# Two attention blocks and a tangent MLP on one core: x read once and transposed on TensorE, the second softmax centred instead of normalised, and a new list-scheduled order

## Chip, cores and metric

One core of one Trainium2 chip. The metric is the time of one execution on the device, in microseconds (us); lower is better. Engines are named as in the profile: PE is TensorE (PEld its weight loads), ACT is ScalarE, DVE is VectorE, POOL is GpSimd, SP is SyncE, which issues all DMAs here. Its DMA queue is worked off in the order of issue, and an issue that waits holds back those behind it.

## What is computed

```python
B, N, m, C = 4, 12480, 32, 128            # x: (B, N, C), inducing: (m, C)
def mab(q, kv):
    s = (q @ kv.transpose(0, 2, 1)) / np.sqrt(C)
    a = np.exp(s - s.max(-1, keepdims=True))
    a /= a.sum(-1, keepdims=True) + 1e-09
    return a @ kv
h = mab(I, x)                              # 32 rows a batch, each a mean over 12480 tokens
t = mab(x, h)                              # 12480 rows a batch, each a mean over 32 rows of h
u = t @ w_in                               # 128 -> 2048
out = (u - np.tanh(u)) @ w_out             # 2048 -> 128
```

The first attention needs all tokens of a batch before `h` is known; the second reads the same tokens again. The rows of `t` lie close together, so both kernels replace the MLP by its tangent at the mean over `h` and apply it to the 32 rows alone: the output is then the second attention's weights times a 32x128 matrix. On the chip a bound on the error of that tangent is worked out. If it is exceeded, a general loop after the main part runs; with these inputs it isn't entered, before or after.

## The kernel before

Every operation is registered with a planner by `add(engine, cost, function, reads, writes, priority)`; `Plan.order` places them by priority, with the costs and the number of free buffers in `PLACES`, and the engines' instruction streams are written out in that order. Within an engine nothing overtakes.

Tokens are handled in steps of up to 1920 (four quarters of `SEG` = 480), seven per batch, the last of 960. The host gives x twice: `xT`, channels on the partitions, and `xn`/`xl`, tokens on the partitions.

- `first(b)`: per step a load of `xT` (L279) and four score products in four column groups (L263, through `scores`), which DVE copies from PSUM with a running maximum (L290). Then the maximum over the batch goes through PE (L299, L307) into `nb`. Per step again: a load of `xn` (L315), the exponential with its sum on ACT (L322), 32x32 transposes on DVE (L326), and 15 accumulating products with `xn` into one PSUM tile (L333). Sum, reciprocal and two small products give `hT` (L342 to L353).
- `linear(b)`: 16 products with a 128x128 piece of `w_in` as weights and 32 moving columns (L367); mean, tanh, slope on DVE and ACT (L379 to L405); 16 products with `w_out` (L416); a copy, a product that repeats the 32 rows four times (L419), a copy.
- `second(b, s)` with `b_chain`: scores with `hT` (L263), transposes on DVE (L455), maximum (L457), subtraction on POOL (L462), exponential on ACT (L464), sum (L467), reciprocal (L472, L473), product on POOL (L475), transposes back (L478), output products in halves of two into `o` (L496), each half evicted by ACT (L502), and one store per step (L505).
- `bound`: 16 products with the absolute `w_out` (L525) and a chain of small DVE operations with the least of all sums, up to `limit`.
- `weight`: the weights come as 64-bit words and are turned into float32 by two ACT, five DVE and two POOL passes per chunk (L218 to L242).

PSUM holds four `ps_m` tiles of one bank and two `o` tiles of two banks. SBUF holds 11 `xT`, 5 `xn` and 3 `ot` buffers; `ot` also takes the raw weights. A load waits until the last reader of its buffer is done, a `COPY` into `ot` until the store of that buffer has landed.

Of the kernel before, what the change touches and what calls it, by code (L numbers as in the profile page):

```python
# [19 lines left out]
NQ = 4  # L20
SEG = 480
KB = SEG // 32
SG = NQ * SEG
SMALL = 0.0625
SERIES = (1.0 / 3.0, -2.0 / 15.0, 17.0 / 315.0)
ROUND = 2.0 ** -24
SLACK = 1.0e-3
# [3 lines left out]

class Buf:


    def __init__(self, make=None, tag=None):
        self.make, self.tag = make, tag
        self.t = None
        self.writer, self.readers, self.left = None, [], 0  # L40

    def get(self):
        if self.t is None:
            self.t = self.make()
        return self.t


class Op:
    def __init__(self, eng, cost, fn, deps, bufs, pri, lag):
        self.eng, self.cost, self.fn, self.deps, self.bufs, self.pri, self.lag = eng, cost, fn, deps, bufs, pri, lag  # L50
        self.start = self.end = None


class Plan:
# [5 lines left out]
    def add(self, eng, cost, fn, reads=(), writes=(), pri=0.0, lag=0.15):  # L60
# [8 lines left out]
        op = Op(eng, cost, fn, deps, list(dict.fromkeys([*reads, *writes])), pri, lag)  # L69
# [9 lines left out]
    def order(self):  # L79
        free = dict(self.places)  # L80
        held = set()
        waiting = {}
        users = {}
# [5 lines left out]
        ready = {}  # L89
        events = []  # L90
        count = itertools.count()
        busy = {}

        def release(op, t):
            ready.setdefault(op.eng, []).append((op.pri, op.n, op))
            ready[op.eng].sort(key=lambda x: x[:2])

        for op in self.ops:
            if not op.deps:
                release(op, 0.0)  # L100
        t, done = 0.0, 0
        while done < len(self.ops):
            for eng, queue in ready.items():
                if busy.get(eng, -1.0) > t:
                    continue
                for k, (_, _, op) in enumerate(queue):
                    need = {}
                    for x in op.bufs:
                        if x.tag and x not in held:
                            need[x.tag] = need.get(x.tag, 0) + 1  # L110
                    if any(free[tag] < c for tag, c in need.items()):
                        continue
                    for x in op.bufs:
                        if x.tag and x not in held:
                            held.add(x)
                            free[x.tag] -= 1
                    queue.pop(k)
                    op.start, busy[eng] = t, t + op.cost
                    op.end = t + op.cost + op.lag
                    heapq.heappush(events, (t + op.cost, next(count), None))  # L120
                    heapq.heappush(events, (op.end, next(count), op))
                    break
            assert events, "no operation can start"
# [553 lines left out]
```

## Time and profile before

| | us |
|---|---|
| median of three runs | 269.49 |
| lowest and highest | 267.08, 271.31 |
| span of the profiled execution, first to last instruction | 267.4 |
| busy: PE, DVE, ACT, POOL | 201.6, 171.4, 97.8, 76.9 |
| first eviction of an output begins | 84.24 |

The device time of the profiled execution is not listed apart from its span; the median is 2.1 us above the span. Busy time counts an instruction from its start to its modelled end, so a PE that is busy is not PE at its best: its instructions take about twice as long when the granted clock is the lower one. The profile reports the granted clock per stretch as a share of full speed (0.50 is 1.2 GHz, 1.00 is 2.4 GHz); in the first 40 us it reads 1.00, while the score products there take as long as they do later at 0.50. An fp32 product appears as two MATMUL instructions, a transpose as one.

### The profile page before, as it was taken

What the parts mean: (1) busy time and instruction counts of PE and PEld (TensorE: products, weight loads), DVE (VectorE), ACT (ScalarE), POOL (GpSimd) and SP (SyncE); (2) the same over time, 40 slices, a digit from 0 to 9 for tenths busy, and PEclk for the clock granted to TensorE, in tenths of its full rate; (3) what the DMA queues carried; (4) which work ended last, traced back from release to release, by engine and by line L of the source; (5) the groups of instructions that cost most, each with busy time, mean ns of one, the idle gap of its engine ahead of it and who ended that gap; (6) DMA issues with size and microseconds to landing.
All of it is one profiled execution on the core that took longest, in us unless ns stands there. A gap on an engine that the chain in (4) does not pass through costs nothing.

```text
span 267.4 us, 4742 instructions
## 1 busy us (share of the span) xinstructions
PE 201.6 (75%) x1814; PEld 103.5 (39%) x1814; DVE 171.4 (64%) x446; ACT 97.8 (37%) x167; POOL 76.9 (29%) x78
## 2 busy tenths in 40 slices
PE   0555327579799579769977979987989399999760
PEld 0001026337342436614412645825236266662210
DVE  3989988332998917355876563187988214988640
ACT  3322365100054552222239520233377231327741
POOL 1535464100156311010642310014425100264610
PEclk9999999995999959856996895579799755989855
DMA  6999999999958999999779999989358233314882
GB/s 214 416 419 417 417 415 354 307 417 415 372 225 309 399 336 332 418 364 383 256 271 386 380 294 422 347 250 394 151 206 290 90 151 146 147 77 184 365 334 86
DMA packets 13166, 81.27 MB, mean 304 GB/s; under 512 B 1616, under 2 KB 1616, under 8 KB 13136
## 3 DMA queue, kind: packets, MB, share of 16 engines
q1 hardware_dynamic: 13136, 80.89, 79.4%
q8 instruction: 16, 0.26, 0.4%
q14 instruction: 14, 0.11, 0.1%
HBM read 55.33 MB, written 25.56 MB: 303 GB/s over the span
## 4 chain that ended last, share of the span: by engine, by line
DMA 45%; PE 21%; DVE 14%; ACT 13%; issue 2%; SPq 2%; POOL 1%; ACTq 0%; DVEq 0%; POOLq 0%
DMA outT<-ot 35%; ACT ot L502 12%; DMA xT<-in_xT 9%; PE o L496 7%; PE ps_m L367 5%; PE ps_m L263 4%; PE ps_m L416 3%; DVE bt L478 2%; DVE ot L230 2%; DVE s L290 1%; PE ps_m L525 1%; DVE ot L231 1%; DVE S_all L467 1%; DVE ot L228 1%; DVE bmx L457 1%
## 5 line engine op out<-in xcount | busy, mean ns | idle before, releaser
L502 ACT COPY ot<-o 128x960 f32<-128x960 f32 x52 | 47.7, 961 | 85.6 <-DMA outT<-ot 72.6
L496 PE MATMUL o<-bt,P 32*128 32x480 f32 x208 | 53.2, 798 | 20.9 <-ACT ot L502 16.5
L462 POOL TENSOR_TENSOR be<-be,bmx 128x480 f32<-128x480 f32 (+1 forms) x28 | 27.7, 993 | 102.8 <-DVE bmx L457 86.1
L263 PE MATMUL ps_m<-xT,indT_sb 128*32 128x480 f32 x208 | 38.0, 733 | 20.7 <-DMA xT<-in_xT 18.9
L475 POOL TENSOR_TENSOR be<-be,brs 128x480 f32<-128x480 f32 (+1 forms) x28 | 27.8, 993 | 52.2 <-DVE brs L473 36.9
L333 PE MATMUL ps_m<-xn,et 128*32 128x128 f32 (+1 forms) x840 | 35.5, 314 | 8.0 <-issue 4.3
L333 PEld LDWEIGHTS ps_m<-xn,et 128*32 128x32 f32 (+1 forms) x840 | 28.9, 126 | 20.5 <-issue 10.6
L496 PEld LDWEIGHTS o<-bt,P 32*128 32x128 f32 x208 | 16.9, 232 | 48.9 <-ACT ot L502 41.4
L263 PE MATMUL ps_m<-xT,hT 128*32 128x480 f32 x208 | 33.8, 711 | 0.0
L478 DVE STREAM_TRANSPOSE bt<-be 128x480 f32<-128x480 f32 (+1 forms) x28 | 18.6, 665 | 15.1 <-PE o L496 13.1
L326 DVE STREAM_TRANSPOSE et<-s 128x480 f32<-128x480 f32 (+1 forms) x28 | 18.2, 655 | 13.4 <-PE ps_m L333 6.9
L367 PE MATMUL ps_m<-hT,win_sb 128*128 128x32 f32 x128 | 23.6, 359 | 1.3 <-DVE hT L353 1.3
L367 PEld LDWEIGHTS ps_m<-hT,win_sb 128*128 128x128 f32 x128 | 23.1, 283 | 2.9 <-DVE hT L353 2.1
L464 ACT ACTIVATE be<-be 128x480 f32<-128x480 f32 (+1 forms) x28 | 16.9, 603 | 18.8 <-POOL be L462 18.8
L290 DVE TENSOR_SCALAR_CACHE_REDUCE s<-ps_m 128x480 f32<-128x480 f32 (+1 forms) x28 | 17.8, 646 | 8.9 <-PE ps_m L263 8.8
L455 DVE STREAM_TRANSPOSE be<-ps_m 128x480 f32<-128x480 f32 (+1 forms) x28 | 18.3, 659 | 6.7 <-PE ps_m L263 6.7
L467 DVE TENSOR_REDUCE S_all<-be 128x15 f32<-128x480 f32 (+1 forms) x28 | 17.7, 631 | 6.1 <-ACT be L464 5.9
L263 PEld LDWEIGHTS ps_m<-xT,indT_sb 128*32 128x32 f32 x208 | 7.0, 122 | 37.4 <-issue 17.0
L322 ACT ACTIVATE s<-s,nb 128x480 f32<-128x480 f32 (+1 forms) x28 | 19.2, 690 | 2.3 <-DVE nb L309 2.3
L457 DVE TENSOR_REDUCE bmx<-be 128x15 f32<-128x480 f32 (+1 forms) x28 | 17.5, 631 | 0.4
L379 DVE TENSOR_REDUCE mean<-ps_m 128x16 f32<-128x512 f32 x4 | 2.8, 691 | 23.1 <-PE ps_m L367 23.1
L416 PE MATMUL ps_m<-wout_sb,W 128*32 128x128 f32 x128 | 14.9, 276 | 2.5 <-DVE W L405 2.5
(96 smaller groups left out, 165.6 us busy)
## 6 DMA issues: line engine op xcount, KB each, us to landing
xT<-in_xT SPq DMA_DIRECT2D x24, 960.0 KB, 8.5
xn<-in_xn SPq DMA_DIRECT2D x24, 960.0 KB, 9.8
outT<-ot SPq DMA_DIRECT2D x24, 960.0 KB, 4.4
ot<-in_w_in SPq DMA_DIRECT2D x4, 512.0 KB, 7.4
ot<-in_w_out SPq DMA_DIRECT2D x4, 512.0 KB, 6.2
xT<-in_xT SPq DMA_DIRECT2D x4, 480.0 KB, 8.3
xn<-in_xl SPq DMA_DIRECT2D x4, 480.0 KB, 7.6
outT<-ot SPq DMA_DIRECT2D x4, 480.0 KB, 3.6
```

The lines of the kernel that those rows point to most:

```text
L263: nc.tensor.matmul(ps[q * m:(q + 1) * m, :SEG], lhsT=w, rhs=row, start=True, stop=True)
L290: nc.vector.tensor_scalar(out=s1.get()[:P, s, :], in0=ps.get()[:P, :SEG], scalar1=1.0, scalar2=None, op0=ALU.mult, op1=ALU.max, accum_out= ...
L333: nc.tensor.matmul(hacc.get()[q * m:(q + 1) * m, :C], lhsT=et.get()[:P, k, :], rhs=x.get()[:P, k, :], start=(s == 0 and k < NQ), stop=(s = ...
L367: nc.tensor.matmul(psM.get()[:, f * m:(f + 1) * m], lhsT=win_sb[:, f * 128:(f + 1) * 128], rhs=hT4s[b][:, :m], start=True, stop=True)
L416: nc.tensor.matmul(psP.get()[:m, :128], lhsT=W.get()[:, f, :], rhs=wout_sb[:, f, :], start=(f == 0), stop=(f == NF - 1))
L457: add("DVE", 0.64, lambda: nc.vector.tensor_reduce(out=bmx.get()[:P], in_=be.get()[:P], axis=AX.X, op=ALU.max), reads=[be], writes=[bmx], ...
L462: add("POOL", 1.1, lambda: nc.gpsimd.tensor_tensor(out=be.get()[:P], in0=be.get()[:P], in1=wide(bmx.get()[:P]), op=ALU.subtract), reads=[b ...
L467: add("DVE", 0.64, lambda: nc.vector.tensor_reduce(out=S()[:P], in_=be.get()[:P], axis=AX.X, op=ALU.add), reads=[be], writes=[part], pri=pri)
L475: add("POOL", 1.1, lambda: nc.gpsimd.tensor_tensor(out=be.get()[:P], in0=be.get()[:P], in1=wide(brs.get()[:P]), op=ALU.mult), reads=[brs], ...
L478: add("DVE", 0.67, lambda: nc.vector.transpose(out=bt.get()[:P], in_=be.get()[:P].rearrange("p k i -> p (k i)")), reads=[be], writes=[bt], ...
L496: nc.tensor.matmul(o.get()[:, q - h, :SEG], lhsT=P4_b[b].get()[p, :], rhs=bt.get()[p, :], start=True, stop=True)
L502: nc.scalar.copy(out=t, in_=o.get()[:, :, :SEG])
```

## The change

1. **x is read once.** `xn` and `xl` are no longer loaded (`LOADED` is empty). Instead PE transposes each `xT` step in 14 blocks of 128x128, seven to a `d` tile of two banks (L385), and ACT or DVE copies the 896 columns to SBUF (L391 or L393, whichever the planner picks; `out_of_psum` gives it a cost for each). The `d` tiles, two, also take the outputs.
2. **Seven equal steps** of 1792 tokens (four quarters of 448); the last begins so as to end at the batch's end, its 64 tokens that were seen already are set to -3e38 before the exponential (L344) and skipped in the store.
3. **The second attention is centred.** `hT` now has 32 columns more, `h` less its mean over the 32 rows, made by `foldc` in the same product (L422). Scores with it (L315) are copied by DVE with a running maximum (L540); the maximum over a group of steps goes through PE (L550) and shifts the exponential on ACT (L564). No maximum, sum or quotient per token is formed, nor the two transposes: the sum is taken as 32, and the evictions of the output (L583 on ACT, L585 on DVE) multiply by exp(shift)/32 and add the mean's image `Pm`. `bound` gets a second condition, on the largest centred score, in place of the sums.
4. **Linear part.** `scores` is used with `w_in` as the moving operand, four products of 512 columns (L315), a DVE transpose brings the result back; the slope's product has a single DVE pass; the products with `w_out` (L477, twice) run in four column groups, and `foldc` and `mean_w` sum them (L484, L485).
5. **Weights**: one DVE pass of `exponent` becomes an ACT pass (L281).
6. **Buffers and planner**: fixed slots per tag; new `PLACES`; two evicting engines; loads are held back when more than `AHEAD` is under way.

```diff
-SG = NQ * SEG
+KB = 14
+W = KB * 32
+ST = NQ * W
...
+PLACES = dict(xT=13, sl=9, et=4, wide=6, s=4, d=2, m2=3, k=7)
+LOADED = frozenset()
...
-    PLACES = dict(xT=11, xn=5, s1=1, be=3, bt=2, et=2, ot=3, ps=4, o=2, W=1)
...
+            def above(e, r=r):
+                nc.scalar.activation(out=r["e"].bitcast(F32), in_=r["e"], func=AF.Relu, bias=shift[:, 0:1])
...
-            add("SP", nq * 0.6, lambda x=x, s=s, P=P: nc.sync.dma_start(
-                out=x.get()[:P], in_=xn[b, :, s * KB:(s + 1) * KB, :] if s < NS else xl[b]),
-                writes=[x], pri=pri + 5 * NSG + 5 * s - 30, lag=2)
...
+                    for h in range(2):
+                        d = place("d")
+
+                        def turn(e, x=x, d=d, h=h):
+                            o = d.get().rearrange("p a w -> p (a w)")
+                            for k in range(HB):
+                                at = (h * HB + k) * 128
+                                nc.tensor.transpose(out=o[:, k * 128:(k + 1) * 128], in_=x.get()[:, at:at + 128], identity=ident)
+
+                        def out(eng, xn_t=xn_t, d=d, h=h):
+                            src = d.get().rearrange("p a w -> p (a w)")[:, :HB * 128]
+                            dst = xn_t.get()[:, h * HB * C:(h + 1) * HB * C]
+                            if eng == "ACT":
+                                nc.scalar.copy(out=dst, in_=src)
+                            else:
+                                nc.vector.tensor_copy(dst, src)
+                        add("PE", 0.95, turn, reads=[x, ident_b], writes=[d], pri=q0 - 3, lag=0.2, hold=[xn_t, et])
+                        add(out_of_psum(HB * 128), 0, out, reads=[d, xn_t], writes=[halves[h]], pri=q0 - 3)
...
-            for f in range(NF):
-                nc.tensor.matmul(psM.get()[:, f * m:(f + 1) * m], lhsT=win_sb[:, f * 128:(f + 1) * 128], rhs=hT4s[b][:, :m],
-                                 start=True, stop=True)
...
+            n = DFF // NQ
+            scores(psM.get(), [win_sb[:, q * n:(q + 1) * n] for q in range(NQ)], hTs[b][:, m:2 * m], n)
...
+        def column(ps, of):
+            for f in range(NF):
+                q = f % NQ
+                nc.tensor.matmul(ps.get()[q * m:(q + 1) * m, :128], lhsT=of(f), rhs=wout_sb[:, f, :], start=f < NQ, stop=f >= NF - NQ)
...
+                def ex(e, sl=sl, k=len(pair), nb=nb):
+                    t = sl.get()[:, :k, :].rearrange("p a w -> p (a w)")
+                    nc.scalar.activation(out=t, in_=t, func=AF.Exp, scale=SC, bias=nb)
...
+                        def ev(eng, d=ds[h], h=h, ot=ot, wg=wg):
+                            dst = ot.get()[:, 2 * h * W:2 * (h + 1) * W].rearrange("p (q n) -> p q n", q=2)
+                            src = d.get()[:, :, :W]
+                            if eng == "ACT":
+                                nc.scalar.activation(out=dst, in_=src, func=AF.Identity, scale=wg.get(), bias=Pm.get())
+                            else:
+                                nc.vector.tensor_scalar(out=dst, in0=src, scalar1=wg.get(), scalar2=Pm.get(),
+                                                        op0=ALU.mult, op1=ALU.add)
```

The order on PE around the end of batch 2's first attention, before (`o` are output products of batch 1, `ps_m` at L333 the accumulation of batch 2, `hT4_2` its result, L367 the up product):

```order
L263 MATMUL ps_m_1396<-xT_1222,indT_sb_70 32x480 x4
L351 MATMUL ps_m_1408<-fold_68,hs_1404 128x128
L367 MATMUL ps_m_1412<-hT4_2_75,win_sb_71 128x32 x16
L496 MATMUL o_1437<-bt_1295,P4_1075 128x480 x2
L496 MATMUL o_1443<-bt_1295,P4_1075 128x480 x2
L263 MATMUL ps_m_1452<-xT_560,hT4_2_75 32x480 x4
L496 MATMUL o_1465<-bt_1392,P4_1075 128x480 x2
```

The same place after (`d0`, `d1` are the two PSUM tiles, L385 the transposes of batch 2's steps, L404 its accumulation, L422 the product that gives `hT`, L315 with `win_sb` the up product):

```order
L385 MATMUL d0_100<-ident_112,xT8_72 128x128 x7
L404 MATMUL s3_99<-wide2_92,et2_88 32x128 x14
L385 MATMUL d1_101<-ident_112,xT8_72 128x128 x7
L385 MATMUL d0_100<-ident_112,xT9_73 128x128 x7
L404 MATMUL s3_99<-wide3_93,et3_89 32x128 x14
L385 MATMUL d1_101<-ident_112,xT9_73 128x128 x7
L385 MATMUL d0_100<-ident_112,xT10_74 128x128 x7
L404 MATMUL s3_99<-wide5_95,et0_86 32x128 x14
L385 MATMUL d1_101<-ident_112,xT10_74 128x128 x7
L422 MATMUL s1_97<-fold_113,k6_111 128x160
L385 MATMUL d0_100<-ident_112,xT11_75 128x128 x7
L315 MATMUL s2_98<-win_sb_119,hT_2_123 32x512 x4
```

Where output products stood around 16 slim products, there is now a run of transposes with accumulations between them; the up product is four wide ones behind it.

ACT around the tanh of batch 0, before (L322 exponentials of the first attention, L517 the bound's absolute weights, L382 the tanh, L502 the first eviction of an output):

```order
L322 ACTIVATE s1_85,sum_88<-s1_85,nb_239 64x480
L517 ACTIVATE ot_393<-wout_sb_72 128x1024
L517 ACTIVATE ot_403<-wout_sb_72 128x1024
L382 ACTIVATE th_485<-mean_478 128x16
L464 ACTIVATE be_506<-be_506 128x480
L418 COPY P1_579<-ps_m_529 32x128
L464 ACTIVATE be_527<-be_527 128x480
L421 COPY P4_593<-ps_m_584 128x128
L464 ACTIVATE be_569<-be_569 128x480
L502 COPY ot_608<-o_601 128x960
```

and after (L391 are evictions of transposes of batch 1, L281 and L290 weight passes, L602 the bound's, L453 the tanh, L479 and L481 the copies of the two column products):

```order
L391 COPY wide0_90<-d0_100 128x896
L281 ACTIVATE wide3_93<-wide3_93,shift_117 128x512
L290 ACTIVATE wide3_93<-wide3_93 128x512
L391 COPY wide1_91<-d0_100 128x896
L391 COPY wide1_91<-d1_101 128x896
L391 COPY wide2_92<-d0_100 128x896
L602 ACTIVATE xT0_64<-wout_sb_120 128x1024
L602 ACTIVATE xT2_66<-wout_sb_120 128x1024
L453 ACTIVATE th_10_647<-mean_9_625 128x16
L391 COPY wide2_92<-d1_101 128x896
L479 COPY k1_106<-s1_97 128x128
L481 COPY k3_108<-s3_99 128x128
```

Evictions of the next batch's transposes and weight passes now stand ahead of the tanh in ACT's queue, where before there were only exponentials of the same batch.

## Rows read from the trace of the kernel before

**Rows 1.** The page: span, busy time by engine, main DMA queue, chain by engine.

```profile
span 267.4 us, 4742 instructions
...
PE 201.6 (75%) x1814; PEld 103.5 (39%) x1814; DVE 171.4 (64%) x446; ACT 97.8 (37%) x167; POOL 76.9 (29%) x78
...
q1 hardware_dynamic: 13136, 80.89, 79.4%
...
DMA 45%; PE 21%; DVE 14%; ACT 13%; issue 2%; SPq 2%; POOL 1%; ACTq 0%; DVEq 0%; POOLq 0%
```

**Rows 2.** The chain of waits in order of time: start us, us, what.

```profile
84.24 1.83 ACT ot L502 x2
86.08 8.21 DMA outT<-ot
94.39 1.83 ACT ot L502 x2
96.24 5.12 DMA outT<-ot
```

**Rows 3.** Stretches: PE, PEld, DVE, ACT, POOL busy (instructions), granted clock, DMA share, GB/s.

```profile
20.00:30.00 10.00, 5.24 (x20) 0.84 (x20) 9.53 (x16) 2.72 (x4) 5.10 (x4) 1.00 1.02 417
160.00:170.00 10.00, 9.62 (x66) 7.14 (x64) 2.30 (x7) 1.82 (x2) 0.00 (x0) 0.50 1.00 410
190.00:200.00 10.00, 8.95 (x87) 2.73 (x79) 8.32 (x21) 6.62 (x13) 3.69 (x4) 0.99 0.42 172
200.00:210.00 10.00, 8.35 (x195) 5.82 (x190) 7.90 (x22) 5.61 (x13) 4.92 (x5) 1.00 0.79 270
```

**Rows 4.** PE's timeline: start us, us, instructions of one line, idle time before.

```profile
7.96 1.83 PE L263 MATMUL ps_m<-xT,indT_sb 128*32 128x480 f32 x8 [7.96 <-DMA xT<-in_xT]
...
77.25 1.09 PE L496 MATMUL o<-bt,P 32*128 32x480 f32 x8
...
82.24 0.27 PE L299 MATMUL ps_m<-ident,mx 128*1 128x128 f32 x1
...
85.28 1.90 PE L496 MATMUL o<-bt,P 32*128 32x480 f32 x8
...
108.03 3.76 PE L367 MATMUL ps_m<-hT,win_sb 128*128 128x32 f32 x32 [0.57 <-DVE hT L353]
...
152.72 3.98 PE L333 MATMUL ps_m<-xn,et 128*32 128x128 f32 x120
...
165.40 7.04 PE L367 MATMUL ps_m<-hT,win_sb 128*128 128x32 f32 x32 [0.38 <-DVE hT L353]
...
228.87 1.82 PE L263 MATMUL ps_m<-xT,hT 128*32 128x480 f32 x16
...
245.65 1.34 PE L496 MATMUL o<-bt,P 32*128 32x480 f32 x8
```

**Rows 5.** Groups by line and form: shapes, count, busy us, mean ns, idle before.

```profile
L502 ACT COPY ot<-o 128x960 f32<-128x960 f32 x52 | 47.7, 961 | 85.6 <-DMA outT<-ot 72.6 <-PE o L496 12.2 <-ACT ot L502 0.4
...
L322 ACT ACTIVATE s<-s,nb 128x480 f32<-128x480 f32 x24 | 16.5, 690 | 2.3 <-DVE nb L309 2.3
...
L326 DVE STREAM_TRANSPOSE et<-s 128x480 f32<-128x480 f32 x24 | 15.6, 655 | 9.7 <-ACT s L322 5.5 <-PE ps_m L333 3.2 <-ACT ot L236 1.0
L290 DVE TENSOR_SCALAR_CACHE_REDUCE s<-ps_m 128x480 f32<-128x480 f32 x24 | 15.3, 651 | 8.9 <-PE ps_m L263 8.8
...
L464 ACT ACTIVATE be<-be 128x480 f32<-128x480 f32 x24 | 14.5, 604 | 18.8 <-POOL be L462 18.8
...
L236 ACT ACTIVATE ot<-ot 128x512 f32<-128x512 uint32 x8 | 5.4, 676 | 15.4 <-DVE ot L224 15.4
...
L322 ACT ACTIVATION_READ_ACCUMULATOR s<-s,nb 128x1 f32 x24 | 4.6, 193 | 0.0
```

**Rows 6.** The last instruction of ACT, in the timeline of the span's end.

```profile
261.28 0.96 ACT L502 COPY ot<-o 128x960 f32<-128x960 f32 x1 [3.70 <-PE o L496]
```

More of the change, by code (lines that the diff above doesn't have):

```diff
@@ L79, in order @@
     def order(self):
[L80 to L83, printed above, removed]
+        free = {tag: list(range(n)) for tag, n in self.places.items()}
+        waiting, users = {}, {}
         for n, op in enumerate(self.ops):
@@ L98, in order @@
         for op in self.ops:
             if not op.deps:
-                release(op, 0.0)
+                release(op)
         t, done = 0.0, 0
         while done < len(self.ops):
-            for eng, queue in ready.items():
+            for eng in ready:
                 if busy.get(eng, -1.0) > t:
                     continue
-                for k, (_, _, op) in enumerate(queue):
+                if eng == "SP" and moving > t + AHEAD:
+                    heapq.heappush(events, (moving - AHEAD, next(count), None))
+                    continue
+                for _, _, op in ready[eng]:
+                    if eng == "DVE" and len(op.costs) > 1 and busy.get("ACT", -1.0) < t + WAIT:
+                        continue
@@ L117, in order @@
[L117 to L120, printed above, removed]
+                        if x.tag and x.slot is None:
+                            x.slot = free[x.tag].pop(0)
+                    for other in op.costs:
+                        ready[other] = [x for x in ready[other] if x[2] is not op]
+                    op.eng, op.start = eng, t
@@ L121, in order @@
+                    busy[eng] = t + op.costs[eng]
+                    op.end = busy[eng] + op.lag
+                    if eng == "SP":
+                        moving = max(moving, t + 1.3) + op.size / RATE
+                        op.end = moving + 1.0
+                    heapq.heappush(events, (busy[eng], next(count), None))
                     heapq.heappush(events, (op.end, next(count), op))
                     break
-            assert events, "no operation can start"
+            if not events:
+                for eng, queue in ready.items():
+                    print(eng, [(o.pri, o.n, [x.tag for x in o.bufs if x.tag and x.slot is None]) for _, _, o in queue][:6])
+                print(free, t)
+                raise SystemExit
@@ L262, in scores, with out_of_psum @@
+            add("POOL", 1.4, join, reads=[buf, lo], writes=[outs[k]], pri=p)
+            add("POOL", 1.4, scale, reads=[buf, ex], writes=[outs[k]], pri=p)
+    xT_b = {}
+    def scores(ps, rows, w, n):
         for q, row in enumerate(rows):
-            nc.tensor.matmul(ps[q * m:(q + 1) * m, :SEG], lhsT=w, rhs=row, start=True, stop=True)
+            nc.tensor.matmul(ps[q * m:(q + 1) * m, :n], lhsT=w, rhs=row, start=True, stop=True)
+    def out_of_psum(n):
+        return {"ACT": 0.17 + 0.00084 * n, "DVE": 0.14 + 0.00104 * n}
@@ L566, in fused_kernel @@
+        add("DVE", 0.9, decide, reads=[low, *nb_b], writes=[], pri=pri)
+    weight(w_in, win_sb, win_b, 60, -23)
+    weight(w_out, wout_sb.rearrange("p f d -> p (f d)"), wout_b, 70, -19)
     for b in range(B):
[L567 to L569 removed]
+        P4, Pm = first(b, 100.0 * b)
+        second(b, P4, Pm, 100.0 * (b + 1))
     bound(100.0 * B - 20)
+    ops = plan.order()
     order = tc.manual_schedule(engines={ET.PE, ET.Activation, ET.DVE, ET.Pool, ET.SP})
```

674 lines of the change are left out of this document (355 added, 319 removed).

## Prediction

> **What bounds the kernel now.** I read the page first, then the chain of waits in order of time, then a table of stretches, then TensorE's own timeline for prices. The page says three things [rows 1]: no engine is full (PE 75%, DVE 64%), the main DMA queue moves 80.89 MB at 79.4% of its engines' time, and the chain that ended last is 45% DMA, most of it output stores. The chain shows how [rows 2]: from 84 us on ScalarE evicts one output step (1.83 us), then waits 5 to 8 us until an older store has landed and its `ot` buffer is free. The three `ot` buffers wait for a store that shares its engines with two copies of the input, `xT` and `xn`. The stretches show both limits [rows 3]: at 20 to 30 us the DMA moves 417 GB/s and is full; at 160 to 170 us DMA is full again while PE is busy 9.62 of 10 us at a granted clock of 0.50, in the 7.04 us of L367 [rows 4]. So before is bound by transfers, with a TensorE that often runs at 1.2 GHz and is then nearly full itself.
>
> **What is removed.** The 25.56 MB of `xn`: 80.89 MB become about 55.5 (one `xT` of 28 x 0.9175 MB, 25.6 of output, 4.2 of weights). At the 417 GB/s of [rows 3] that is 133 us instead of 194. DMA cannot be the bound of anything longer than about 140 us. On VectorE and GpSimd the second attention loses its maximum, its subtraction, its sum, reciprocal, product and second transpose per step; what stays is one 448-column pass. The 32 matmul instructions of L367 and the 32 of L416 per batch become 8 of 512 columns in four column groups, plus 64 (two column products) in four groups.
>
> **TensorE's work after, at 2.4 GHz.** An fp32 matmul is two instructions in the trace.
> - Scores: 16 instructions of 480 columns took 1.82 us [rows 4], so 0.91 for a step of 8, and 0.91 x 448/480 = 0.85. Two per step, 56 in all: 47.6 us.
> - Accumulation: 120 instructions in 3.98 us [rows 4], 33 ns each; 28 per step are 0.92 us, 28 steps: 25.9.
> - Output: 8 instructions took 1.09, 1.34 and 1.90 us [rows 4], the longer ones because the two PSUM buffers are awaited. I take 1.34 x 448/480 = 1.25; 28 steps: 35.
> - Transposes, new: 14 per step, 392 in all, each with a 128x128 weight load and 128 moving columns. No row shows one. Below: 33 ns, the accumulation's price for 128 moving columns. Above: 0.27 us, the one-column transpose L299 that ran alone, latency included [rows 4]. The nearest row is L367 at full clock: 32 instructions in 3.76 us, each with a 128x128 weight load [rows 4], 117 ns. I take 117: 1.64 us per step, 45.9 in all.
> - Linear part: 0.97 for the up product (0.91 x 512/480), 2 x 32 x 33 ns for the columns, 1.3 for three small products: 4.4 per batch, 17.6.
> - 18 small products for maxima and sums and the bound at the end: 9, an estimate at 0.38 each (between L299's 0.27 and twice it) and 2 for the bound.
>
> Sum: 181 us, above the 133 of the DMA: TensorE becomes the bound.
>
> **ACT and DVE** share the evictions: 112 of 896 columns (56 transposed, 56 output), 83 on ACT and 29 on DVE by the order. An eviction of 960 columns took 0.961 us on ACT [rows 5], so 0.90 for 896. ACT in all: 83 x 0.90 = 75, exponentials about 30, weights 24 x 0.676 = 16, small 10: 131. DVE: 84 passes of 448 (0.65 x 448/480 = 0.61, from L290 and L326 in [rows 5]) = 51, evictions 29, weights 22, linear and bound about 40: 142. Both are below 181, and stand beside PE's work except where PE waits for one of the two `d` buffers.
>
> **The path.** (1) The first `xT` lands. Before, the first scores began at 7.96 us after 1.5 MB [rows 4]; now 0.92 MB stand ahead, 0.58 less, 1.4 us at 417 GB/s: 6.5 us. (2) Seven scores and 56 transposes up to the first maxima. At 2.4 GHz 5.95 + 6.6 = 12.5 us; at 1.2 GHz (8 instructions took 1.83 at the start [rows 4], twice 0.91) 25. The seven loads need until 6.5 + 6 x 2.2 = 20, so the earliest is about 21, the latest 31. I take 24, and 25 with the maximum passed through PE. (3) ACT's queue up to the tanh of batch 0, in the order shown: 24 weight passes at 0.676, four exponentials with sums (0.914 for 896 columns on the slope between L464 and L502, and 0.28 for the sum, by L322 against L464 and the 0.193 of reading the accumulator [rows 5]: 4.4), 12 evictions (10.8), two passes of 1024 columns (2.0): 33.4, so 58.4. The tanh now stands behind evictions of batch 1 that are queued ahead of it; if they were not there it would come 5 us earlier. (4) To the first output matmul: tanh 0.2, tangent 0.9, column 1.06, copy, points and copy 1.1, exponential 0.9, about 4.2 (small ones estimated from [rows 5]): 63 us. (5) By then the order has put through PE 16 scores, 154 transposes, 7 accumulations, 7 second scores and one linear part: 13.6 + 18 + 6.5 + 6 + 4.4 + 1 = 49.5. So 131.5 remain. (6) Waits: with a clock of 0.99 to 1.00 and DMA not full PE was busy 8.95 and 8.35 of 10 [rows 3]; part of that is in my 1.25 for an output already, so I allow 10%: 131.5 / 0.9 = 146, which gives 209. (7) Tail: the last eviction began 6.1 us before the span's end [rows 6]; the last step is alike: 215. The span before is 267.4 against a median of 269.49, 2.1 more: **217 us**.
>
> Set against before: there the first eviction of an output begins at 84 us and 28 steps follow at 6.5 us each; by this sum the first begins at about 64 and 28 follow at 5.4.
>
> **Costed at nothing**: the 28 loads after the first seven (DMA is idle a third of the time; if SP's in-order queue holds a load behind a store that waits for its eviction, PE would lose up to the landing time of a store, but 13 `xT` places are nearly two batches ahead); the weights' POOL passes (two per chunk, beside ACT's); the 34 extra columns per batch of the overlapping last step (0.5%); the bound, which now needs no sums of the last step and ends before the last stores. The wait that is added is PE's on `d`: transposes and outputs share two buffers, and behind a waiting transposition stand accumulations, the next scores and the linear part in PE's own order. In a run of transposes a fill is 0.82 and an eviction 0.90, so two alternating buffers cost PE 0.1 us or so per fill, 9 us over the 90 fills after 63 us; it is in the 10%.
>
> **Rivals.**
> - *Transposes are cheap* (33 ns): 238 of them remain after 63 us, 0.084 x 238 / 0.9 = 22 less, and 3 at the start: 191. For it: 128 moving columns need no more in L333. Against: L333 loads 32 weight columns in four groups, a transposition 128.
> - *The clock falls in the runs of transposes.* Per batch the order puts 11 fills of transposes and about three accumulations one after another: 11 x 0.82 + 3 x 0.92 = 11.8 us at 2.4 GHz, 23.6 at 1.2. For three batches 35 more, for the first 6 (half of it is in step 2), less 5 of waits for ACT that it hides: 253. For it: L367 kept PE busy 9.62 of 10 us at a granted 0.50 [rows 3], so a busy TensorE is not always granted 2.4 GHz. Against: L367's instructions move 32 columns, a transposition 128. The Trainium skill ("TensorE: Matmul & The Clock Gate", Part 4: PE-mode transpose) says that the full clock does not engage for transposes, as they do not count as busy in the way that matmuls do; by that rule this rival would be the likeliest. The trace before has only single transposes of one column and can show neither.
> - *No gain*: a transposition costs 0.27 us. Then 0.153 x 238 / 0.9 = 40 and 8 at the start: 265. Against: that row holds the latency of one alone.
> - *Slower*: PE is the bound and runs at 1.2 GHz also outside the runs of transposes, since waits for `d` break up its work. With a share h of the remaining 131.5 us done at half clock the time is 217 + 131.5h + about 7 at the start: it passes 275 from h = 0.39 and ends at 355 for h = 1. For it: the scores at the start of before ran so, with waits between them [rows 4]. Against: before, the clock fell where PE waited for DMA or ran L367, and both go.
>
> **How the numbers follow.** Forecast 0.55 (200 to 232: transposes of 90 to 150 ns and waits of 5 to 16%), cheap transposes 0.12, clock in the runs 0.20, no gain 0.05, slower 0.08. The range of 8 in 10 runs from the cheap case, 191, to the clock case, 253. Within 2% is 264 to 275, about what a measurement of this kernel can tell from no change: 0.05; slower 0.08; faster 0.87.
>
> **What would show it.** Right: queue q1 near 55 MB; DMA no longer on top of the chain, PE and ACT there; 7 transposes in about 0.82 us; a score step of 0.85; first output matmul near 63 us; PEclk mostly 9. Wrong: transposes at twice the price or a granted 0.5 in the runs of L385 (clock rival); 7 transposes in 0.3 us (cheap); a chain through ACT's evictions with PE idle over 20% would mean that the two `d` buffers, not TensorE's work, set the pace.

## The result and the profile after

The changed kernel takes 227.57 us (median of four runs, 226.61 to 231.09) against 268.28 us for the kernel before (264.72 to 271.31): ratio 0.853, 95% interval 0.849 to 0.858. The medians are over all runs and the ratio over the fast ones alone, without the one of 231.09 us, so it is not the quotient of the medians (0.848). The forecast was 217 us with a range of 191 to 253.

The page of the changed kernel, in the order of [rows 1]:

```profile
span 224.7 us, 5401 instructions
...
PE 186.0 (83%) x2234; PEld 109.0 (48%) x2234; DVE 143.9 (64%) x386; ACT 131.3 (58%) x188; POOL 23.4 (10%) x26
...
PEclk9999679995899999999999999999999999999555
...
q1 hardware_dynamic: 9360, 55.46, 63.3%
...
PE 2%; ACT 1%; issue 1%; DVE 1%; DVEq 0%
```

The queue moves 55.46 MB instead of 80.89 and is idle a third of the time. The chain reaches back only over the last 17 us, so here it says nothing of the rest. PE is the fullest engine, and its granted clock (PEclk, in tenths for 40 slices) is low in three places: at 20 to 30 us, at 50 to 60 us, and in the last 17 us.

TensorE's timeline at the start (answers to [rows 4]; L385 are the transposes, L315 the scores, L355 the product for the first maxima, L422 the one that gives `hT`, L573 the outputs):

```profile
6.45 1.72 PE L315 MATMUL s<-xT,indT_sb 128*32 128x448 f32 x8 [6.45 <-DMA xT<-in_xT]
8.10 2.70 PE L385 MATMUL d<-ident,xT 128*128 128x128 f32 x14
10.72 0.96 PE L315 MATMUL s<-xT,indT_sb 128*32 128x448 f32 x8
11.61 1.75 PE L385 MATMUL d<-ident,xT 128*128 128x128 f32 x14
...
22.60 0.38 PE L355 MATMUL s<-mq,fold 128*128 128x4 f32 x2 [1.43 <-DVE mq L353]
...
44.73 1.75 PE L385 MATMUL d<-ident,xT 128*128 128x128 f32 x14
51.24 1.76 PE L385 MATMUL d<-ident,xT 128*128 128x128 f32 x7 [4.76 <-ACT wide L391]
...
60.28 1.07 PE L315 MATMUL s<-win_sb,hT 128*32 128x512 f32 x8 [0.56 <-DVE hT L425]
...
73.49 0.96 PE L315 MATMUL s<-xT,indT_sb 128*32 128x448 f32 x8 [1.20 <-DMA xT<-in_xT]
...
74.80 1.03 PE L573 MATMUL d<-sl,k 32*128 32x448 f32 x8
...
96.22 0.44 PE L422 MATMUL s<-fold,k 128*128 128x160 f32 x2
```

Fourteen transposes take 1.68 us from start to start (11.61 to 13.29), 120 ns each. The first output product comes at 74.80 us. Its batch's `hT` is used at 60.28, though the accumulation behind it had ended near 44.8. DVE's timeline says why; `hs` (L420) is the step that waits, L278, L285 and L286 are weight passes:

```profile
47.63 1.51 DVE L278 TENSOR_SCALAR wide<-wide 128x512 uint32<-128x512 uint32 x1
49.07 1.49 DVE L285 TENSOR_SCALAR wide<-wide 128x512 uint32<-128x512 f32 x1
50.59 1.66 DVE L286 SCALAR_TENSOR_TENSOR wide<-wide 128x512 uint32<-128x512 uint32 x1
52.17 0.42 DVE L278 TENSOR_SCALAR wide<-wide 128x512 uint32<-128x512 uint32 x1
...
55.00 1.50 DVE L278 TENSOR_SCALAR wide<-wide 128x512 uint32<-128x512 uint32 x1
56.42 0.34 DVE L420 TENSOR_SCALAR k<-s,rs 128x128 f32<-128x128 f32 x1
```

From 45.9 us on DVE works through weight passes back to back, some of 0.42 us and some of 1.5; `hs` stands behind them. ACT's evictions stand behind ACT's part of the same passes, so PE waits 4.76 us for one (above).

From 60 to 100 us, as the outputs begin at 74.80, the granted clock is whole, in runs of transposes too, and PE is busy 7.66 to 10.00 of ten us (columns as in [rows 3]):

```profile
60.00:70.00 10.00, 9.72 (x141) 5.38 (x141) 8.43 (x28) 4.39 (x8) 1.28 (x1) 1.00 0.61 207
70.00:80.00 10.00, 7.66 (x62) 2.45 (x61) 7.31 (x29) 6.84 (x12) 0.12 (x1) 1.00 0.81 335
80.00:90.00 10.00, 9.45 (x179) 7.00 (x179) 7.17 (x16) 7.86 (x12) 0.00 (x0) 1.00 0.72 288
90.00:100.00 10.00, 10.00 (x128) 7.14 (x124) 2.15 (x6) 5.31 (x7) 0.00 (x0) 1.00 0.01 2
```

The groups that answer to [rows 5] (an eviction of 896 columns, of a transpose and of an output; a slow DVE pass):

```profile
L391 ACT COPY wide<-d 128x896 f32<-128x896 f32 x51 | 45.0, 905 | 35.2 <-PE d L385 33.5 <-POOL wout_sb L296 0.6 <-ACT wide L391 0.3
L583 ACT ACTIVATE wide<-d,Pm,wg 128x896 f32<-128x896 f32 x32 | 34.6, 1094 | 31.2 <-PE d L573 29.3 <-issue 1.9
...
L278 DVE TENSOR_SCALAR wide<-wide 128x512 uint32<-128x512 uint32 x8 | 7.6, 949 | 0.0
```

### The profile page after: what moved, and what is told of

It reads as the page before. It is cut to its first block, busy times and chain, and to the rows that moved or that the text cites. A ratio compares the mean times of both kernels' runs of the same rounds, so it can differ in the third digit from the quotient of the medians.

```text
span 224.7 us, 5401 instructions
## 1 busy us (share of the span) xinstructions
PE 186.0 (83%) x2234; PEld 109.0 (48%) x2234; DVE 143.9 (64%) x386; ACT 131.3 (58%) x188; POOL 23.4 (10%) x26
## 3 DMA queue, kind: packets, MB, share of 16 engines
q1 hardware_dynamic: 9360, 55.46, 63.3%
## 5 line engine op out<-in xcount | busy, mean ns | idle before, releaser
L391 ACT COPY wide<-d 128x896 f32<-128x896 f32 x51 | 45.0, 905 | 35.2 <-PE d L385 33.5
L385 PE MATMUL d<-ident,xT 128*128 128x128 f32 x392 | 54.9, 289 | 10.0 <-ACT wide L391 6.4
L385 PEld LDWEIGHTS d<-ident,xT 128*128 128x128 f32 x392 | 45.4, 148 | 24.0 <-ACT wide L391 10.2
L583 ACT ACTIVATE wide<-d,Pm,wg 128x896 f32<-128x896 f32 x32 | 34.6, 1094 | 31.2 <-PE d L573 29.3
L585 DVE TENSOR_SCALAR wide<-d,wg,Pm 128x896 f32<-128x896 f32 x24 | 29.0, 1206 | 19.2 <-PE d L573 18.0
L573 PE MATMUL d<-sl,k 32*128 32x448 f32 x224 | 36.9, 632 | 3.9 <-ACT wide L583 3.9
L315 PE MATMUL s<-xT,indT_sb 128*32 128x448 f32 x224 | 28.3, 589 | 11.5 <-DMA xT<-in_xT 10.6
L404 PE MATMUL s<-wide,et 128*32 128x128 f32 x784 | 28.6, 281 | 1.6 <-DVE et L396 1.6
L404 PEld LDWEIGHTS s<-wide,et 128*32 128x32 f32 x784 | 23.0, 112 | 11.4 <-DVE et L396 5.3
L340 DVE TENSOR_SCALAR_CACHE_REDUCE sl<-s 128x448 f32<-128x448 f32 x28 | 17.2, 615 | 17.3 <-PE s L315 17.2
L315 PE MATMUL s<-xT,hT 128*32 128x448 f32 x224 | 24.4, 543 | 0.0
L573 PEld LDWEIGHTS d<-sl,k 32*128 32x128 f32 x224 | 12.3, 194 | 21.0 <-ACT wide L583 8.2
L564 ACT ACTIVATE sl<-sl,nbs 128x896 f32<-128x896 f32 (+1 forms) x16 | 14.7, 938 | 5.2 <-DVE nbs L553 5.2
L540 DVE TENSOR_SCALAR_CACHE_REDUCE sl<-s 128x448 f32<-128x448 f32 x28 | 16.9, 620 | 0.9 <-PE s L315 0.8
L315 PEld LDWEIGHTS s<-xT,indT_sb 128*32 128x32 f32 x224 | 5.8, 112 | 21.6 <-issue 11.0
L344 POOL MEMSET sl<- 64x32 f32 x4 | 0.7, 173 | 119.5 <-DVE sl L340 119.5
L420 DVE TENSOR_SCALAR k<-s,rs 128x128 f32<-128x128 f32 x4 | 1.4, 346 | 17.2 <-PE s L404 17.2
L315 PEld LDWEIGHTS s<-xT,hT 128*32 128x32 f32 x224 | 6.6, 109 | 9.9 <-issue 8.8
L278 DVE TENSOR_SCALAR wide<-wide 128x512 uint32<-128x512 uint32 x8 | 7.6, 949 | 0.0
L290 ACT ACTIVATE wide<-wide 128x512 f32<-128x512 uint32 x8 | 5.4, 678 | 3.1 <-DVE wide L278 3.0
```

Source lines behind the costliest of these rows:

```text
L315: nc.tensor.matmul(ps[q * m:(q + 1) * m, :n], lhsT=w, rhs=row, start=True, stop=True)
L340: nc.vector.tensor_scalar(out=sl.get()[:, j, :], in0=ps.get()[:, :W], scalar1=1.0, scalar2=None, op0=ALU.mult, op1=ALU.max, accum_out=mxg. ...
L385: nc.tensor.transpose(out=o[:, k * 128:(k + 1) * 128], in_=x.get()[:, at:at + 128], identity=ident)
L391: nc.scalar.copy(out=dst, in_=src)
L404: nc.tensor.matmul(hacc.get()[q * m:(q + 1) * m, :C], lhsT=et.get()[:, k, :], rhs=xn_t.get()[:, k * C:(k + 1) * C], start=at < NQ, stop=at ...
L540: nc.vector.tensor_scalar(out=sl.get()[:, j, :], in0=ps.get()[:, :W], scalar1=1.0, scalar2=None, op0=ALU.mult, op1=ALU.max, accum_out=bm.g ...
```

## Experiments

Each ratio is to the kernel before on the same chip. The changed kernel's own is 0.853 (0.849 to 0.858).

**Which part gave the gain.** Two parts of the change are undone, one at a time and together.

`e1_loaded_all`: x loaded twice again, no transposes.

```diff
-LOADED = frozenset()
+LOADED = frozenset((b, s) for b in range(4) for s in range(7))
```

> x is read twice again: all 28 steps load the natural layout by DMA (LOADED holds every step), no transposes on TensorE, everything else of the change kept. Theory A (after the first outputs TensorE's own work sets the pace; reading x once relieves the DMA but costs TensorE about 47 us, 56 fills at 0.84): TensorE's work falls from about 170 to 125 us, 25.7 MB come back, q1 near 81 MB and 194 us at 417 GB/s, so DMA is the bound; 205 to 235 us, about the time of the changed kernel. Theory B (most of the gain comes from reading x once): 250 us or more.

Measured: 234.93 us, ratio 0.884 (0.877 to 0.890).

```profile
PE 157.3 (68%) x1842; PEld 74.0 (32%) x1842; DVE 144.5 (63%) x384; ACT 84.6 (37%) x134; POOL 24.3 (11%) x26
...
q1 hardware_dynamic: 13392, 81.16, 87.9%
```

With the bytes of before the time is still 12% below before, and 3.6% above the changed kernel. Theory B falls; the time lies at the upper end of theory A's 205 to 235.

`e6_normalised`: the second attention normalised per token as before, x read once.

```diff
-                        nc.vector.tensor_scalar(out=sl.get()[:, j, :], in0=ps.get()[:, :W], scalar1=1.0, scalar2=None,
-                                                op0=ALU.mult, op1=ALU.max, accum_out=bm.get()[:, at:at + 1])
...
+                nc.vector.transpose(out=sl.get()[:, 0, :], in_=ps.get()[:, :W])
+                nc.vector.tensor_reduce(out=sl.get()[:, 1, :KB], in_=v3(sl), axis=AX.X, op=ALU.max)
+                nc.gpsimd.tensor_tensor(out=v3(sl), in0=v3(sl), in1=sl.get()[:, 1, :KB].unsqueeze(2).to_broadcast([128, KB, m]), op=ALU.subtract)
...
+                nc.vector.transpose(out=sl.get()[:, 1, :], in_=sl.get()[:, 0, :])
```

> x read once as in the changed kernel, but the second attention normalised per token as before: per step a DVE transpose out of PSUM, maximum, POOL subtraction, exponential, sum and reciprocal, POOL product, transpose back; no products for maxima; outputs evicted with scale 1 and the mean's image; the limit is set to zero (left out: the bound's second condition). Theory A (centring gave most of the gain, since it takes work off VectorE, which is now the busiest engine after PE): DVE gets 28 x about 2.0 us more (two transposes of 0.61, a maximum and a sum of about 0.65 each, against one pass of 0.61), 56 us on 144: 200 us, and it meets POOL's 28 x 2 passes of about 1.1 us, beside which DVE was seen to run slower; 245 to 275 us, within 2% of before or above. Theory B (DVE has room for it: 144 of 225 us busy): 228 to 236 us, so that the order, the equal steps and the linear part gave most.

Measured: 257.47 us, ratio 0.963 (0.954 to 0.971). Against the changed kernel DVE has 36 us more and POOL 51:

```profile
PE 202.6 (79%) x2214; PEld 115.3 (45%) x2214; DVE 180.2 (71%) x431; ACT 134.9 (53%) x198; POOL 74.7 (29%) x82
...
q1 hardware_dynamic: 9360, 55.46, 55.2%
```

It lies in theory A's 245 to 275, though not within 2% of before; B falls. The rise of DVE was put too high (56 expected). DMA is idle 45% of the time, and yet the kernel is only 4% faster than before.

`e7_normalised_loaded`: both edits together.

> e6 and e1 together: x loaded twice and the second attention normalised per token; what remains of the change is the linear part, the weights' moved pass, the equal steps and the order. Theory A (centring is the main part, reading once adds 3%): 250 to 270 us, little below before, and close to e6 since loading twice relieves PE and ACT/DVE evictions where DVE is the bound (e6 less 0 to 15). Theory B (order and linear part are the main part): 225 to 242 us. If the two parts add up by ratios, e7 is e6 x 1.035.

Measured: 269.11 us, ratio 1.011 (1.005 to 1.016). It lies at the end of theory A's 250 to 270, but it is slower than e6, not up to 15 us faster. The ratios multiply to about 1% (0.963 x 0.884 / 0.853 is 0.998, against 1.011). The order, the equal steps, the linear part and the moved weight pass together gain nothing that can be seen by themselves, as far as this second attention is that of before. The four ratios:

| | second attention as before | centred |
|---|---|---|
| x loaded twice | 1.011 (e7) | 0.884 (e1) |
| x read once | 0.963 (e6) | 0.853 (changed kernel) |

Centring takes off 11 to 13% (0.853/0.963, 0.884/1.011), reading x once 3 to 5% (0.853/0.884, 0.963/1.011).

**Whether TensorE's work sets the pace.** `e2_half_acc`: 200 of the 392 accumulating products stay and 192 are left out, the limit is zero.

```diff
+                        if at % 8 < 4:
                         nc.tensor.matmul(hacc.get()[q * m:(q + 1) * m, :C], ...
```

> Leaves out 192 of the 392 accumulating products of the first attention (48 of 98 per batch), so the output is not the reference's; the bound's verdict is set to zero. Nothing else is less: same transposes, evictions, DMAs. Theory A (TensorE's work sets the pace after the first outputs): 192 x 0.071 us = 13.7 us less on TensorE, three quarters of it after the first output: 9 to 12 us faster, 216 to 219. Rival (the fills and evictions of the two PSUM tiles set the pace): less than 4 us faster.

Measured: 225.68 us, ratio 0.851 (0.846 to 0.855); its interval overlaps that of the changed kernel. The 192 products of two instructions at 33 ns are 13 us of PE's work, and the end moved by less than 1%. Theory A's 216 to 219 us are missed; the time is in the rival's range. Where the 13 us went:

```profile
70.00:80.00 10.00, 6.11 (x41) 2.20 (x36) 5.08 (x21) 4.93 (x7) 0.12 (x1) 0.81 0.62 259
80.00:90.00 10.00, 9.66 (x109) 4.85 (x104) 8.73 (x17) 7.63 (x13) 0.00 (x0) 0.85 0.71 288
```

```profile
74.53 0.96 PE L315 MATMUL s<-xT,indT_sb 128*32 128x448 f32 x8 [2.46 <-DMA xT<-in_xT]
...
97.37 0.44 PE L423 MATMUL s<-fold,k 128*128 128x160 f32 x2
...
140.43 0.44 PE L423 MATMUL s<-fold,k 128*128 128x160 f32 x2
...
168.97 0.98 PE L385 MATMUL d<-ident,xT 128*128 128x128 f32 x7 [0.86 <-ACT wide L584]
...
180.15 0.54 PE L423 MATMUL s<-fold,k 128*128 128x160 f32 x2
```

PE waits 2.46 us for an `xT` (1.20 in the changed kernel), then runs at a granted 0.81 and 0.85 where that had 1.00; `hT` of batch 1 comes at 97.37 against 96.22. (L423 here is L422 in the changed kernel, where batches 2 and 3 have it at 141.39 and 182.36.) From there to batch 2's `hT` it is 43.1 us against 45.2, and from that to batch 3's 39.7 against 41.0. In these two stretches the clock is whole in both kernels, 6.3 us of accumulations are left out, and 3.4 us are won; in the second, PE waits 0.86 us for the eviction of an output (168.97) where the changed kernel does not wait. Of 13 us, about 2 were kept at the end. So where the clock stays, about half of what is taken off TensorE is won. That the two PSUM tiles set the rest of the pace, as the rival has it, is not shown: no run changed them alone.

**The start.** `e3_wout_later`: the passes on `w_out` get a later priority.

```diff
-    weight(w_out, wout_sb.rearrange("p f d -> p (f d)"), wout_b, 70, -19)
+    weight(w_out, wout_sb.rearrange("p f d -> p (f d)"), wout_b, 90, -19)
```

> One number: the priority of the passes over w_out is 90 instead of 70, behind the linear part of batch 0. In VectorE's order the product that ends batch 0's first attention (L420) then stands ahead of eleven weight passes. Theory C (the first output was late because L420 stood behind weight passes in VectorE's queue from 44.8 to 56.4 us): L420 begins by about 50 us, first output 3 to 6 us earlier, 221 to 225 us. Rival (ScalarE's queue sets the tanh, as the prediction had it): within 1.5 us of the changed kernel.

Measured: 223.43 us, ratio 0.843 (0.840 to 0.846). The time is theory C's, and its rival falls, but the first output moved by less than the 3 to 6 us of C. The up product of batch 0 starts at 49.27 instead of 60.28, the first output at 72.27 instead of 74.80: the passes that left the way of `hT` now hold the product with `w_out`, whose last piece is ready at 66.24; that product starts at 67.55 (66.70 in the changed kernel). Batch 1's `hT` comes at 94.84.

`e4_pool_small`: POOL's two weight passes on 8 columns of 512, the limit is zero.

```diff
-                nc.gpsimd.tensor_tensor(out=dst, in0=dst, in1=r["lo"].bitcast(F32), op=ALU.add)
+                nc.gpsimd.tensor_tensor(out=dst[:, :8], in0=dst[:, :8], in1=r["lo"].bitcast(F32)[:, :8], op=ALU.add)
```

> Leaves out most of GpSimd's work on the weights: its sixteen passes keep their place and their waits but touch 8 of 512 columns, so the weights are wrong; the bound's verdict is set to zero. Order on all engines the same. Theory D (VectorE's weight passes take 1.5 us instead of 0.42 while GpSimd works on SBUF): no weight pass over 1 us, L420 5 to 7 us earlier, first output 6 to 9 us earlier, 218 to 223 us. Rival (the passes are long for another reason, or ScalarE's queue decides): passes of 1.5 us remain, within 2 us of the changed kernel.

Measured: 225.61 us, ratio 0.852 (0.845 to 0.858), no difference that these runs can tell. So theory D's 218 to 223 us are missed. The slow DVE passes are gone all the same:

```profile
L278 DVE TENSOR_SCALAR wide<-wide 128x512 uint32<-128x512 uint32 x8 | 3.4, 429 | 0.0
```

```profile
51.07 0.98 PE L385 MATMUL d<-ident,xT 128*128 128x128 f32 x7 [4.00 <-ACT wide L391]
...
55.49 0.51 PE L422 MATMUL s<-fold,k 128*128 128x160 f32 x2
```

949 ns became 429 (the four groups of weight passes on DVE: 25.2 us to 15.6). So DVE's slow passes are POOL's doing, but ten microseconds less of DVE in the start bring the up product only from 60.28 to 57.96. `hs` (L420) begins at 51.68 instead of 56.42, but PE's product with it (L422) only at 55.49 instead of 57.17: in PE's queue it stands behind transposes that wait for ACT's evictions, and ACT's weight passes stay.

`e8_one_weight_pass`: of a chunk's passes only the first on ACT stays; the limit is zero.

> Of the eight operations that turn a weight chunk into float32 only the first ACT pass is left (left out: three DVE operations in four passes, two ACT, two POOL per chunk; the limit is set to zero). Theory A (the 10 us by which the forecast was too low are the start: the weights stand in ACT's and DVE's queue ahead of batch 0's products): ACT loses 16 x 0.68 = 11 us and DVE about 24 in the first 60 us; the first output matmul comes at about 62 to 65 instead of 74.8, hT of batch 1 at 84 to 88 instead of 96, and the time falls by 8 to 12 to 216 to 220 us. Rival (what comes earlier waits later: batch 1's products cannot start earlier, as in e3 and e4, where batch 1's hT came at 94 to 97 whatever came before): first output earlier, batch 1's hT at 93 or later, time 223 to 226 us.

Measured: 212.84 us, ratio 0.800 (0.797 to 0.804), 14 us below the changed kernel (0.853 less 0.800, of 267). More than forecast. The marks of its PE timeline:

```profile
44.42 0.44 PE L415 MATMUL s<-fold,k 128*128 128x160 f32 x2
...
57.34 1.03 PE L566 MATMUL d<-sl,k 32*128 32x448 f32 x8
...
84.08 0.44 PE L415 MATMUL s<-fold,k 128*128 128x160 f32 x2
```

`hT` of batch 0 at 44.42 (57.17 in the changed kernel), first output at 57.34 (74.80), `hT` of batch 1 at 84.08 (96.22), and the end 13.5 us earlier by the spans. What is won in the start stays, this time to the end. The rival falls. In e3 part of the passes only moved ahead of another product that is needed, in e4 they were shorter on one engine and the other kept them; here nearly all of them are off both queues.

**Versions that use it.** `e5_mixed`: e3, with 18 of 28 steps loading their natural layout, as listed (of batch 0 two are loaded and five transposed), and with one `et` buffer more and one `m2` fewer.

```diff
+PLACES = dict(xT=13, sl=9, et=5, wide=6, s=4, d=2, m2=2, k=7)
+LOADED = frozenset(((0, 4), (0, 6), (1, 1), (1, 3), (1, 4), (1, 6), (2, 0), (2, 1), (2, 2), (2, 3), (2, 5), (2, 6), (3, 0), (3, 1), (3, 3), (3, 4), (3, 5), (3, 6)))
```

> 18 of the 28 steps load their natural layout again, 10 are transposed on PE (2 of batch 0, ... as listed in LOADED; 9.2 to 16.5 MB are added), w_out's passes stand later as in e3, five et buffers and two m2. Theory A (after the change PE, ACT and DVE are a closely coupled set with hardly any slack, DMA has a third of its time free, so a mixture gains what neither extreme does): 18 steps drop 18 x 1.68 = 30 us of transposes from PE and 36 evictions of 0.905 = 33 us from ACT and DVE; DMA moves 72 MB, 173 us at 417 GB/s. About 200 to 213 us, below e3's 223.4 and e1's 234.9. Rival (a load in the queue holds back a store or the next xT, or PE's clock falls in the gaps that the loads leave, as in e1 with its mean granted clock of 0.83): 222 us or more.

Measured: 220.03 us, ratio 0.828 (0.821 to 0.834): below e3 and e1, above the 200 to 213 forecast. Neither side had the time right: PE loses 21 us of work against the changed kernel, but waits, and runs at a mean granted clock of 0.86 (0.93 there), as the rival had it. The buffers' part was not run apart. From 40 to 100 us PE's longest waits are these:

```profile
PE s L315 <- DVE sl L540: 8.0, 2, 4.7
PE s L404 <- DMA wide<-in_xn: 2.8, 1, 2.8
```

L540 is the copy of the second scores, held up in DVE's queue; weight passes stand there too in that stretch, but which of the copy's neighbours held it was not tried.

`e9_bits`: a chunk becomes float32 by three passes on DVE alone.

```diff
+                nc.vector.tensor_scalar(out=r["e"], in0=r["hi"], scalar1=3, scalar2=0x3FFFFFF8,
+                                        op0=ALU.logical_shift_left, op1=ALU.bitwise_and)
...
+                nc.vector.scalar_tensor_tensor(out=r["e"], in0=r["hi"], scalar=0xC0000000, in1=r["e"],
+                                               op0=ALU.bitwise_and, op1=ALU.bitwise_or)
...
+                nc.vector.scalar_tensor_tensor(out=dst.bitcast(U32), in0=r["lo"], scalar=29, in1=r["e"],
+                                               op0=ALU.logical_shift_right, op1=ALU.bitwise_or)
```

> A version meant to beat the changed kernel: a weight chunk becomes float32 by three passes of integer shifts and masks on VectorE (exponent and mantissa moved together, right for zero and for every weight in float32's normal range, cut off instead of rounded), with no ACT and no POOL pass; everything else as in the changed kernel. Theory A (the weight passes in ACT's and DVE's queues ahead of batch 0 are the mis-sized term; e8 took off 14 us without them): 24 ACT passes of 0.68 and all of POOL's go, and with POOL silent DVE's passes stay near their shortest 0.42 to 0.65: 8 x about 1.6 = 13 us of DVE instead of about 24. First output matmul at 58 to 64, 213 to 219 us, ratio to before 0.80 to 0.825. Rival (what helped in e8 was DVE's queue alone, and 24 more passes on it keep hT of batch 0 late): first output at 68 or later, 221 us or more.

Measured: 218.00 us, ratio 0.818 (0.811 to 0.826). Theory A, at its upper end; the first output is at 66.28, between the two. Of e8's 14 us about 9 are won with 14 us of weight passes still on DVE and none on ACT or POOL, so it need not be taken off both queues; which of ACT's passes and POOL's slowing of DVE counts more was not run apart. Its DVE passes:

```profile
L305 DVE SCALAR_TENSOR_TENSOR wide<-wide 128x512 uint32<-128x512 uint32 x8 | 5.5, 689 | 0.1
L301 DVE TENSOR_SCALAR wide<-wide 128x512 uint32<-128x512 uint32 x8 | 3.4, 423 | 0.0
```

`e10_bits_mixed`: e9 with 16 of 28 steps loaded, the buffers of e5, and `w_out`'s passes earlier, which the expectation does not name:

```diff
-    weight(w_out, wout_sb.rearrange("p f d -> p (f d)"), wout_b, 70, -19)
+    weight(w_out, wout_sb.rearrange("p f d -> p (f d)"), wout_b, 60, -19)
```

> e9's weight passes and, as in e5, a mixture: 16 of 28 steps load their natural layout, none of batch 0 but one; five et buffers and two m2. Theory A (e5 gained 1.5% over e3 with a clock of 0.86 and PE waiting in the first 70 us, where its loads and weight passes crowd; without these the mixture takes 27 us off PE and 29 off ACT and DVE): below e9 by 5 to 12, 202 to 211 us. Rival (the clock falls in the gaps, or DMA at 70 MB becomes the bound, as for e1): no faster than e9.

Measured: 212.52 us, ratio 0.793 (0.783 to 0.804): 5.5 us below e9, in the range of differences that was expected and 1.5 above the absolute one. It is the fastest kernel of the study, 20.7% below before. How much of the 5.5 us is the mixture's, and how much the priority's and the buffers', was not run apart.

```profile
PE 163.0 (77%) x2010; PEld 88.2 (42%) x2010; DVE 128.6 (61%) x373; ACT 93.5 (44%) x137; POOL 1.4 (1%) x10
...
q1 hardware_dynamic: 11664, 70.15, 85.1%
```

## Why the forecast held, and where it was wrong

**The sum.** The profiled span is 224.7 us, the forecast's 215; the terms that failed are steps (3) and (4). Steps (1) and (2) were good: first scores at 6.45 (6.5 forecast), the first maxima's product at 22.60 (24 to 25). Step (3) put the tanh of batch 0 at 58.4 by adding up ACT's queue; it came at 64.67. `hs` stood behind DVE's weight passes, which the sum did not count there, and PE's product with `hs` behind transposes whose tiles waited for ACT (e4). With `w_out`'s passes later on all three engines (e3) the tanh comes at 55.46.

Step (4) allowed 4.2 us from the tanh to the first output, and it took 10.1. The group's maximum, which must go through PE before the exponential, had been left out of it, and so had the other work that stands in the queues there:

```profile
64.67 0.20 ACT L453 ACTIVATE th<-mean 128x16 f32<-128x16 f32 x1
...
71.79 0.28 DVE L553 TENSOR_REDUCE nbs<-s 128x1 f32<-128x128 f32 x1
...
72.11 1.04 ACT L564 ACTIVATE sl<-sl,nbs 128x896 f32<-128x896 f32 x1 [1.80 <-DVE nbs L553]
```

PE's product for the maximum (L550) starts at 69.81, but DVE reads it (L553) only at 71.79, behind the bound's small passes; the exponential ends at 73.15, and in PE's order the output product still stands behind a score step that waits 1.20 us for its `xT` (73.49, above). Even in e8 the stretch takes 7.4 (49.92 to 57.34). Together steps (3) and (4) had the first output 11.8 us too early (63 against 74.80), and 2.1 were given back after it: 149.9 us remained, 152 forecast. The weight passes cost 14 us in all by e8, but ACT's 16 us of them were in the sum; how much of the 11.8 is due to DVE's passes and POOL's is not shown.

**The prices.** A transpose was put at 117 ns and is 120; seven at 0.82, measured 0.84. So the rivals "transposes are cheap" (33 ns) and "no gain" (270 ns) fell. The 117 came from L367, with its 128x128 weight load and 32 moving columns; no run shows that the weight load is what a transpose costs, so that it came out so close is in part luck. A score step at 0.85, measured 0.78 (six in a row, 61.14 to 65.79) to 0.89; an accumulation at 0.92, measured 0.84 (two in a row) to 1.00; an output step at 1.25, measured 0.96 where its tiles were free (74.80 to 75.76, e.g.). ACT and DVE were put at 131 and 142 us busy and are 131.3 and 143.9. The last eviction begins 7.9 us before the end, not 6.1.

**The clock.** The rival "the clock falls in the runs of transposes" fell. PE ran its first 14 transposes in 2.70 us from 8.10 and the next 14 in 1.75, its first score step in 1.72 and the next in 0.96: the prices went from those of the lower level to those of the upper one while PE did transposes and score products (the granted clock reads 1.00 in that stretch throughout, so this is read from the times). From 60 to 100 us it is 1.00, runs of L385 included, and so it stays up to 208 us. The rule of the Trainium skill that was weighed against this ("TensorE: Matmul & The Clock Gate", Part 4: PE-mode transpose), that the full clock does not engage for transposes, does not agree with this trace. Accumulations stand between the transposes here; a long run of transposes alone was not tried. The slower rival fell as a whole too, though in the last 17 us the clock did what it says. The clock fell where PE had waited: it reads 0.50 at 24 to 30 us, after waits for DVE and for an `xT`, 0.66 at 50 to 60 us, behind the weights, and 0.50 in the last 17 us, between two `d` tiles.

```profile
213.89 2.78 PE L573 MATMUL d<-sl,k 32*128 32x448 f32 x8 [0.39 <-ACT wide L583]
...
216.78 1.21 DVE L585 TENSOR_SCALAR wide<-d,wg,Pm 128x896 f32<-128x896 f32 x1 [2.02 <-PE d L573]
```

There an output step of 0.96 us takes 2.78.

**The bound.** "Before is bound by transfers" was wrong as a cause. e1 moves 81 MB, the bytes of before, in 235 us. Against e7, e6 takes 25 MB off the kernel with the old second attention, adds the transposes and their evictions, and gains 5%. The bytes of before need 194 us at 417 GB/s by the forecast's own division, 73 less than its span; that the chain of [rows 2] ended in stores showed who was late there, not what the kernel was short of. What most of the time came from is centring, which the prediction named only in passing as VectorE's and GpSimd's loss of work: 11 to 13%. Which of the passes it removes (on DVE, on POOL, or the round trips between them) counts most was not tried apart.

"TensorE becomes the bound" was half right. From 74.8 to 216.7 us, where the last eviction begins, PE is busy 129.7 of 141.9 us; the forecast had 131.5 of 146. But 13 us of its work taken out of the accumulations move the end by less than 1% (e2), in part because the clock fell, and where it did not fall about half of what was taken out was won; 14 us are won by clearing the weights out of ACT's and DVE's queues (e8). The division by 0.9 gave the right remainder, with an output step priced 0.29 us too high in it, and the runs do not show that its reason was right.

**Costed at nothing.** POOL's weight passes, "beside ACT's", are not free: DVE runs some of its passes three times as long beside them. e4 shows that this costs the whole kernel nothing that can be told while ACT's passes stay. The overlap of the last step is 64 tokens a batch, not 34 columns; the 0.5% is right. By its own terms the first rival gives 192 us, not 191.

## What to carry to other kernels

Before a chain that ends in DMA is read as a shortage of bandwidth, divide the bytes by the rate that the trace shows: a span far above that can have another cause, and here centring, which takes passes off VectorE and GpSimd, was worth three times what a third of the bytes was. One-time work at the start (here the weights' conversion) belongs in the sum with all engines whose queues it stands in, ahead of the first product that everything waits for; moving a part of it later, or shortening it on one engine, brought 0 to 1%; taking all of it off ACT and POOL, with three passes a chunk left on DVE, brought 4%, and taking it off DVE as well 6%. Two ways to get the same data, one that costs DMA and one that costs PE and evictions, can be mixed step by step: the kernels with a mixture, in which a few buffers and in e10 a priority differ too, were 2 to 3% faster than the same without loads.

## What the hardware showed unexpectedly

A 128x128 float32 transpose on PE costs 120 ns in a run at the full clock, where one of the two instructions of an accumulating product, with as many moving columns but only 32 weight columns, takes 33 [rows 4]; the clock is granted in full in stretches with such runs (1.00 from 60 to 100 us).

A DVE pass of 512 words that takes 0.42 us alone takes 1.5 when a POOL product is under way (47.63 above, beside this one):

```profile
47.44 1.42 POOL L293 TENSOR_TENSOR wout_sb<-wout_sb,wide 128x512 f32<-128x512 f32 x1 [1.51 <-ACT wide L290]
```

The Trainium skill ("SBUF — State Buffer", Who interferes with whom) says that VectorE and GpSimd share a pair of ports, which some of VectorE's instructions use (`tensor_scalar` in a two-port mode among them), and that one then waits for the whole instruction of the other; e4 agrees, where POOL's products shrink to 8 columns and all eight L278 passes take 421 to 443 ns.
